# Reordered weight stores and reloads, and an output layer that runs product by product, in a chunked-attention and maxout kernel

## The chip, the cores and the metric

The kernel runs on one core of a Trainium2 chip. The metric is the device time of one execution in microseconds (us), the median of several runs.

The core's engines are named as in the profile: PE (TensorE, matrix products; PEld is its weight load), DVE (VectorE), ACT (ScalarE), POOL (GpSimd) and SP (SyncE). Here SP issues all DMAs, in the order in which they stand in its queue. Each engine works through its own instructions in order, and waits on semaphores for the others.

## The reference

Attention within chunks of 64 positions, for 8 batches, 8 heads, 576 positions and a head dimension of 64; then a maxout layer on all 4608 tokens:

```python
scores = scale * np.matmul(q_c, k_c.transpose(0, 1, 2, 4, 3))
scores = scores - np.max(scores, axis=-1, keepdims=True)
attn = np.exp(scores)
attn = attn / (np.sum(attn, axis=-1, keepdims=True) + 1e-09)
out = np.matmul(attn, v_c)
...
x = np.ascontiguousarray(attn_out.transpose(0, 2, 1, 3)).reshape(B * S, H * D)
...
h = np.maximum(np.maximum(x @ w1, x @ w2), x @ w3)
return (h @ w_out).astype(np.float32)
```

x is 4608 x 512, the hidden width is 768, and the output is 4608 x 512. All is float32.

## The kernel before

**Tiles, groups, units.** The tokens are 36 tiles of 128. The first two groups of four tiles each (`GROUPS`) go through the maxout layer directly, with the weights in SBUF. The other 28 tiles are four units of 7, 8, 7 and 6 tiles (`UNITS`). A unit's tokens are cut into two halves of `count * 64` columns (448, 512, 448, 384).

**Precision.** Each float32 operand is split into a high part, rounded to the matmul's format (`high`, a copy on ACT), and a low part, the difference (`low`, a subtraction on DVE). A product is three matmuls: low by high, high by low, high by high (`product`, L585).

**Seven products.** In a unit, each product of 2 x 2 blocks is made with seven products instead of eight, in the manner of Strassen and Winograd. The operands of the seven are sums and differences of blocks. Those of the weights are made once, during the second group: `store` (L352) for the nine hidden sets, `store_out` (L405) for the three pairs of blocks of the output weights. Both sum on POOL, split on ACT and DVE, and write the originals and the mixed operands to DRAM. Those of the tokens are made per unit: `operands` (L503) for products 1, 2, 5, 6, 7 and `last_operands` (L509) for 3 and 4, into the rooms X1 to X7.

**A unit on PE.** Nine hidden sets (`hidden`, L593), each for two blocks of 128 hidden columns and one of the three weight matrices: seven products in `ORDER` = 1, 6, 5, 2, 7, 3, 4, each of two steps of three matmuls. The results are combined and their maxima over the three matrices kept in M. After every third set the operands Y of the output layer are made from M (L622 to L637). Then comes the output layer (`project`, L644): for each half mm (128 of the 256 output rows of a block), the seven products over three pairs of blocks jp, nine matmuls each; in the first half the steps of products 1, 6 and 5 are interleaved.

**Banks.** There are five PSUM banks for these products. Product 2 goes on accumulating in the bank of product 1, 7 in that of 6, and 3 in that of 5 (`banks_of_product`, L583). So PE may begin product 2 only when the bank's content after product 1 has been read out, and likewise for 7 and 3. In both layers `combine` (L563) has ACT read out 1, 6 and 5 (into `kept`) and 2, and DVE the sums of 7, 3 and 4; POOL makes two further sums.

**Streamed weights.** A set's weights come back from DRAM into two rooms of the ring: originals, 768 KB (`first`, L513), and mixed operands, 1024 KB (`second`, L517). The first room holds the operands of products 1, 2 and 4, the second those of 5, 6, 7 and 3. There are two rooms of each kind, so that set n + 2 is loaded into the rooms of set n. Both loads are planned for just after set n. The output weights come in seven pieces of 768 KB (`load_outer`, L523), each with two successive products of one half, in contiguous rows; pieces 4 to 6 and the next unit's first two sets are loaded during the output layer, each behind every second product (`loads_within`, L873).

**The order of work.** All queues are written out by hand. `FIRST` orders the first group. From then on a clock `now` advances with every step of PE by an assumed duration (`STEP_H`), and every other piece of work has a due time (`plan`, L773); it enters its engine's queue when the clock reaches it (`passed`, L765). The due times set the order only. The steps that matter below: `operands(u + 1, 6.5)` puts the next unit's token operands 6.5 to 15.9 us behind the start of the output layer, `last_operands` comes behind its end, `tiles` (L835) spreads the attention of the unit after next (three PE pieces V, S, T per tile, softmax on the other engines), the first of them `lead` = 20 us behind the start of the output layer.

**Rooms.** `y_room` (L539) places the 21 operands Y. Those of the last pair for products 7, 3 and 4 lie in rooms X3 and X4. `ao` are four rotating rooms for results, each stored to `out_t` by SP.

Of the kernel before, what the change touches and what calls it, by code (L numbers as in the profile page):

```python
# [30 lines left out]
ORDER = (1, 6, 5, 2, 7, 3, 4)  # L31
SOFTMAX = (("mx", 1.0), ("sub", 1.9), ("exp", 2.8), ("sum", 3.8), ("eps", 4.7), ("rec", 4.9), ("nrm", 5.3))
# [30 lines left out]
def chunk_attn_maxout_kernel(  # L63
# [288 lines left out]
    def store(n):  # L352
# [18 lines left out]
        def sum_of(k, x, y, op):  # L371
            def fn():
                if k == 0:
                    st["c"] = att.tile([P, 4, 256], F32, name="c", tag="rv", bufs=1)
                nc.gpsimd.tensor_tensor(out=st["c"][:, k], in0=x(), in1=y(), op=op)
            return fn

        def high():
            st["s"] = xp.tile([P, 2, 4, 256], F32R, name="s", tag=("xh0", "xl0")[n % 2])
            nc.scalar.copy(out=st["s"][:, 0], in_=st["c"])  # L380

        def low():
            nc.vector.tensor_tensor(out=st["s"][:, 1], in0=st["c"], in1=st["s"][:, 0].bitcast(F32), op=minus)  # L383
# [14 lines left out]
        return [(0.0, whole(0, a)), (1.1, whole(1, b)), (2.2, sum_of(0, a21, a22, plus)),  # L398
                (2.9, sum_of(1, sums(0), a11, minus)), (3.6, sum_of(2, a11, a21, minus)),
                (4.3, sum_of(3, a12, sums(1), minus)), (5.3, high), (6.5, low), (9.2, mixed)]  # L400

    place = {i: p for p, i in enumerate(ORDER)}
    outer_w = {}

    def store_out(jp):  # L405
# [24 lines left out]
        def high():  # L430
            st["h"] = late["hold"].tile([P, 4, 256], F32R, name="sh", tag="k0", bufs=1)
            nc.scalar.copy(out=st["h"], in_=st["c"])

        def low():
            st["l"] = late["hold"].tile([P, 4, 256], F32R, name="sl", tag="k1", bufs=1)
            nc.vector.tensor_tensor(out=st["l"], in0=st["c"], in1=st["h"].bitcast(F32), op=minus)

        def to(first, step, many, m, h):
            w = outer_w["w"].rearrange("p (m i j h x) -> p m i j h x", m=2, i=7, j=3, h=2)
            return w[:, m, first:first + step * (many - 1) + 1:step, jp, h]  # L440

        def originals():
            if jp == 0:
                outer_w["w"] = dram.tile([P, 14 * 768], F32, name="wo")
            for h, src in enumerate((woh, wol)):
                for m in range(2):
                    cols = slice(m * P, (m + 1) * P)
                    nc.sync.dma_start(out=to(0, 3, 2, m, h), in_=src[:, j:j + 2, cols].bitcast(F32))
                    cols = slice(256 + m * P, 256 + (m + 1) * P)
                    nc.sync.dma_start(out=to(6, 1, 1, m, h), in_=src[:, j + 1:j + 2, cols].bitcast(F32))  # L450

        def mixed():
            for h, src in enumerate("hl"):
                for m in range(2):
                    cols = slice(m * P, (m + 1) * P)
                    for half in range(2):
                        nc.sync.dma_start(out=to(1 + 3 * half, 1, 2, m, h),
# [511 lines left out]
```

## Time and profile before

| | us |
|---|---|
| median of 3 runs | 634.1 |
| lowest and highest | 631.84, 634.71 |
| the profiled execution: its time | 635.71 |
| its span, first to last instruction | 633.9 |
| DVE busy | 446.6 |
| ACT busy | 277.1 |
| POOL busy | 295.1 |

The profile is of one execution, at full granted clock of TensorE. A row of a timeline gives start, duration, engine, line, operation, output and inputs, and in brackets the idle time before it and what ended it. A row of groups gives count, busy time, mean duration in ns, and the idle time before these instructions with its releasers. A row of windows gives the stretch, then the busy time of PE, PEld, DVE, ACT and POOL with their counts of instructions, the clock, the busy share of the DMA engines and the GB/s that they moved. A DMA row gives the count, the size of one and the median time from issue to landing. The units' places in time: unit 0's hidden sets start at 178.38 us and its output layer at 277.01; the output layers of units 1, 2 and 3 start at 400.87, 515.01 and 608.35.

### The profile page before, as it was taken

How to read it: one execution, taken by the hardware profiler on the slowest of the kernel's cores; microseconds unless marked ns; L12 is line 12 of the kernel's file. 1: busy time of each engine (PE TensorE's matmuls, PEld its weight loads, DVE VectorE, ACT ScalarE, POOL GpSimd, SP SyncE). 2: the span in 40 equal slices, each digit the busy share in tenths (PEclk: the TensorE clock that was granted, in tenths of full speed). 3: DMA queues.
4: the chain of work that ended last, by engine and by line, in shares of the span. 5: the costliest groups of instructions: out<-in, count | busy, mean ns of one | idle time of the engine just before them, and what ended most of it. 6: DMA issues, size and time to landing. Idle time of an engine off the chain costs nothing.

```text
span 633.9 us, 12714 instructions
## 1 busy us (share of the span) xinstructions
PE 614.7 (97%) x5101; PEld 532.6 (84%) x5102; DVE 446.6 (70%) x676; ACT 277.1 (44%) x491; POOL 295.1 (47%) x243
## 2 busy tenths in 40 slices
PE   7899999999999799999999999999999999899997
PEld 3888877878888678999887888888999999899997
DVE  5889854788856786679549596985488567366761
ACT  4888633454534334444434343443243353332341
POOL 2423577765465654356335352552354346243441
PEclk9999999999999999999999999999999999999999
DMA  8988559576958999378774655678665569766675
GB/s 330 362 297 292 199 184 356 205 254 231 347 172 270 300 311 363 120 267 292 292 269 176 245 204 216 226 279 274 269 236 181 202 230 310 269 228 238 233 255 192
DMA packets 52042, 161.26 MB, mean 254 GB/s; under 512 B 5264, under 2 KB 21392, under 8 KB 46224
## 3 DMA queue, kind: packets, MB, share of 16 engines
q1 hardware_dynamic: 51984, 160.45, 70.6%
q8 instruction: 40, 0.66, 0.4%
q14 instruction: 18, 0.15, 0.1%
HBM read 128.97 MB, written 31.46 MB: 253 GB/s over the span
## 4 chain that ended last, share of the span: by engine, by line
PE 73%; DVE 12%; DMA 8%; ACT 4%; issue 2%; POOL 1%; SPq 0%; POOLq 0%; ACTq 0%; DVEq 0%
PE pm L590 55%; DMA ring<-w 5%; PE pm L172 4%; PE pm L173 4%; PE pm L174 4%; PE s L257 2%; DVE X L501 2%; PE tp L245 2%; PE s L222 2%; DMA wo<-sh 2%; DVE e L232 1%; DVE s L383 1%; DVE mx L227 1%; DVE sm L180 1%; ACT e L236 1%
## 5 line engine op out<-in xcount | busy, mean ns | idle before, releaser
L590 PE MATMUL pm<-X,ring 128*128 128x448 f32 (+2 forms) x1584 | 330.8, 365 | 10.1 <-DMA ring<-w 7.6
L590 PEld LDWEIGHTS pm<-X,ring 128*128 128x128 f32 x1584 | 289.6, 188 | 40.8 <-ACT kept L568 3.5
L568 ACT COPY kept<-pm 128x448 f32<-128x448 f32 (+2 forms) x132 | 69.6, 533 | 141.7 <-PE pm L590 114.2
L590 PE MATMUL pm<-Y,ring 128*128 128x448 f32 (+2 forms) x432 | 91.7, 364 | 0.0
L575 POOL TENSOR_TENSOR kept<-kept 128x448 f32<-128x448 f32 (+2 forms) x44 | 55.7, 1266 | 72.2 <-ACT kept L568 71.8
L590 PEld LDWEIGHTS pm<-Y,ring 128*128 128x128 f32 x432 | 79.4, 188 | 7.8 <-DVE Y L626 0.5
L601 DVE TENSOR_TENSOR most<-pm,most 128x448 f32<-128x448 f32 (+2 forms) x72 | 44.6, 620 | 45.7 <-PE pm L590 44.8
L172 PE MATMUL pm<-xh,wl 128*128 128x512 f32 (+1 forms) x156 | 60.8, 390 | 0.0
L189 POOL TENSOR_TENSOR e<-e,sm 128x512 f32<-128x512 f32 x26 | 28.1, 1081 | 67.3 <-DVE sm L186 50.7
L173 PE MATMUL pm<-xl,wh 128*128 128x512 f32 (+1 forms) x156 | 58.4, 374 | 0.3 <-DVE xl L268 0.3
L174 PE MATMUL pm<-xh,wh 128*128 128x512 f32 (+1 forms) x156 | 58.4, 375 | 0.0
L579 POOL TENSOR_TENSOR kept<-kept 128x448 f32<-128x448 f32 (+2 forms) x24 | 30.8, 1283 | 47.8 <-DVE kept L571 42.3
L626 DVE TENSOR_TENSOR Y<-most,Y 128x448 fp32r<-128x448 f32 (+2 forms) x60 | 49.9, 850 | 3.5 <-ACT Y L623 2.9
L571 DVE TENSOR_TENSOR kept<-pm,kept 128x448 f32<-128x448 f32 (+2 forms) x44 | 27.2, 617 | 34.3 <-PE pm L590 30.0
L623 ACT CAST Y<-most 128x448 fp32r<-128x448 f32 (+2 forms) x60 | 33.3, 568 | 23.0 <-DVE most L601 16.0
L227 DVE TENSOR_REDUCE mx<-s 128x8 f32<-128x512 f32 x36 | 24.6, 683 | 22.9 <-PE s L222 22.9
L250 ACT COPY xs<-tp 128x512 f32<-128x512 f32 x36 | 21.0, 584 | 39.4 <-PE tp L245 39.3
L232 DVE TENSOR_TENSOR e<-s,mx 128x512 f32<-128x512 f32 x36 | 24.8, 690 | 17.8 <-ACT stage L271 17.4
L236 ACT ACTIVATE e<-e 128x512 f32<-128x512 f32 x36 | 22.8, 632 | 29.3 <-DVE e L232 29.3
L174 PEld LDWEIGHTS pm<-xh,wh 128*128 128x128 f32 x156 | 29.3, 188 | 5.5
L172 PEld LDWEIGHTS pm<-xh,wl 128*128 128x128 f32 x156 | 29.4, 188 | 5.4
L571 DVE TENSOR_TENSOR pm<-pm,kept 128x448 f32<-128x448 f32 (+2 forms) x48 | 30.1, 627 | 5.2 <-PE pm L590 4.2
(98 smaller groups left out, 859.6 us busy)
## 6 DMA issues: line engine op xcount, KB each, us to landing
ring<-w SPq DMA_DIRECT2D x36, 1024.0 KB, 6.7
ring<-w SPq DMA_DIRECT2D x36, 768.0 KB, 4.7
ring<-wo SPq DMA_DIRECT2D x28, 768.0 KB, 5.3
buf<-in_qk SPq DMA_DIRECT2D x36, 512.0 KB, 6.6
buf<-in_vb SPq DMA_DIRECT2D x36, 256.0 KB, 6.0
w<-s SPq DMA_DIRECT2D x9, 1024.0 KB, 5.4
stage<-in_w SPq DMA_DIRECT2D x7, 512.0 KB, 5.0
out_t<-ao SPq DMA_DIRECT2D x16, 224.0 KB, 4.6
```

The costliest lines, as they stand in the source:

```text
L172: nc.tensor.matmul(out=o, lhsT=al, rhs=bh, start=first, stop=False)
L173: nc.tensor.matmul(out=o, lhsT=ah, rhs=bl, start=False, stop=False)
L174: nc.tensor.matmul(out=o, lhsT=ah, rhs=bh, start=False, stop=last)
L227: nc.vector.tensor_reduce(out=st["mx"].rearrange("p (g c) -> p c g", c=2), in_=st["s"], axis=AX.X, op=ALU.max)
L232: nc.vector.tensor_tensor(out=st["e"].rearrange("p g c k -> p c g k"), in0=st["s"], in1=most.unsqueeze(3).broadcast_to([P, 2, 4, 64]), op= ...
L568: return lambda: nc.scalar.copy(out=kept(k), in_=o[i])
L571: return lambda: nc.vector.tensor_tensor(out=out(), in0=o[i], in1=kept(k), op=plus)
L575: (0.95, lambda: nc.gpsimd.tensor_tensor(out=kept(2), in0=kept(2), in1=kept(0), op=plus))],
L590: nc.tensor.matmul(out=o[i], lhsT=a, rhs=b, start=new and k == 0, stop=last and k == 2, skip_group_check=i in banks_of_product)
L601: return lambda: nc.vector.tensor_tensor(out=M(k, c), in0=of(), in1=M(k, c), op=most)
L623: return lambda: nc.scalar.copy(out=y_room(i, jp)[:, 0, :half], in_=t[i]())
L626: return lambda: nc.vector.tensor_tensor(out=y_room(i, jp)[:, 1, :half], in0=t[i](), in1=y_room(i, jp)[:, 0, :half].bitcast(F32), op=minus)
```

## The change

- Hidden weights lie in DRAM by product, in the order of the products, high beside low. The first room now holds the operands of products 1, 6 and 5, the second those of 2, 7, 3 and 4. Set n + 2 is loaded into the first room behind product 5 of set n, into the second behind product 4.
- `store` writes its originals in rows of 1 KB and its mixed operands in two DMAs instead of one; `store_out` uses five DMAs per pair of blocks instead of twelve, the mixed one with rows of 8 KB.
- The output layer runs product by product in the order `OUTER`, each for both halves m in turn. A piece of output weights holds one product for all three pairs and both halves, in three rows of 2 KB per partition, and each piece's room is loaded anew behind its own product.
- In the output layer ACT reads out 1, 2 and 6; DVE makes the sums of 7, 5, 3 and 4; POOL makes one sum per half. In the hidden layer the combination is as before, written out in `hidden`.
- The operands Y of the last pair lie in other rooms than X3 and X4; `last_operands` is merged into `operands`, and so falls into the output layer (due 15.95 to 18.3 us behind its start). `lead` is 18 instead of 20.
- The order in which the Y operands are made behind a third set is changed: that of product 2 first.

```diff
+OUTER = (1, 2, 6, 7, 5, 3, 4)
...
         def originals():
             stored[n] = dram.tile([P, 14 * 256], F32, name=f"w{n}")
-            for k, src in enumerate((wh[a][:, w], wl[a][:, w])):
-                nc.sync.dma_start(out=stored[n][:, k * 512:(k + 1) * 512], in_=src.bitcast(F32).rearrange("p c x -> p (c x)"))
-            for k, src in enumerate((wh[b][:, w, 2:], wl[b][:, w, 2:])):
-                nc.sync.dma_start(out=stored[n][:, 1024 + k * 256:1280 + k * 256],
-                                  in_=src.bitcast(F32).rearrange("p c x -> p (c x)"))
+            for h, src in enumerate((wh[a], wl[a])):
+                nc.sync.dma_start(out=to()[:, 0:4:3, h], in_=src[:, w].bitcast(F32).rearrange("p (c k) x -> p c (k x)", c=2))
+            for h, src in enumerate((wh[b], wl[b])):
+                nc.sync.dma_start(out=to()[:, 6, h], in_=src[:, w, 2:].bitcast(F32).rearrange("p c x -> p (c x)"))
 
         def mixed():
-            nc.sync.dma_start(out=stored[n][:, 1536:], in_=st["s"].bitcast(F32).rearrange("p a k x -> p (a k x)"))
+            for k in range(2):
+                nc.sync.dma_start(out=stored[n][:, 512 + 1536 * k:1536 + 1536 * k],
+                                  in_=st["s"][:, 2 * k:2 * k + 2].bitcast(F32).rearrange("p i h x -> p (i h x)"))
...
             for h, src in enumerate((woh, wol)):
-                for m in range(2):
-                    cols = slice(m * P, (m + 1) * P)
-                    nc.sync.dma_start(out=to(0, 3, 2, m, h), in_=src[:, j:j + 2, cols].bitcast(F32))
-                    cols = slice(256 + m * P, 256 + (m + 1) * P)
-                    nc.sync.dma_start(out=to(6, 1, 1, m, h), in_=src[:, j + 1:j + 2, cols].bitcast(F32))
+                nc.sync.dma_start(out=to()[:, 0:2, h], in_=src[:, j:j + 2, :256].bitcast(F32))
+                nc.sync.dma_start(out=to()[:, 6, h], in_=src[:, j + 1, 256:].bitcast(F32))
 
         def mixed():
-            for h, src in enumerate("hl"):
-                for m in range(2):
-                    cols = slice(m * P, (m + 1) * P)
-                    for half in range(2):
-                        nc.sync.dma_start(out=to(1 + 3 * half, 1, 2, m, h),
-                                          in_=st[src][:, 2 * half:2 * half + 2, cols].bitcast(F32))
+            nc.sync.dma_start(out=to()[:, 2:6].rearrange("p i h x -> p (i h x)"),
+                              in_=st["s"].bitcast(F32).rearrange("p i h x -> p (i h x)"))
...
-                    (8.3, high(7)), (9.4, low(7))]
-
-        def last_operands():
-            return [(0.0, high(3)), (1.0, low(3)), (1.1, high(4)), (2.2, low(4))]
+                    (8.3, high(7)), (9.4, low(7)), (9.45, high(3)), (10.6, low(3)), (10.7, high(4)), (11.8, low(4))]
...
-                elif p < 4:
-                    pool, tag = ((att, "qs"), (att, "rv"), (late["hold"], "k0"), (late["hold"], "k1"))[p]
+                elif p in (2, 4):
+                    if "k" not in Y:
+                        Y["k"] = late["hold"].tile([P, 2, 2, HALF], F32R, name="Y", tag="k0", bufs=1)
+                    Y[i, jp] = Y["k"][:, p // 2 - 1]
+                elif p == 5:
+                    Y[i, jp] = Y["woh"][:, 0]
+                elif p == 6:
+                    Y[i, jp] = Y[1, 2]
                 else:
-                    Y[i, jp] = rooms["X"]((3, 3, 4)[p - 4])[:, :, (0, 1, 0)[p - 4]]
+                    pool, tag = {0: (att, "qs"), 1: (att, "rv"), 3: (hpool, "h0")}[p]
...
-                after[4] += [(0.2, less(nc.vector, t[5], lambda: M(0, 1), lambda: M(0, 0))), (0.22, t6),
-                             (1.7, less(nc.gpsimd, t[7], lambda: M(1, 1), lambda: M(0, 1))), (2.3, high(6)), (2.6, low(6)),
-                             (2.9, high(5)), (3.4, low(5)), (4.0, high(2)), (4.6, low(2)), (4.7, high(7)), (5.3, low(7)),
-                             (5.35, less(nc.gpsimd, t[4], lambda: M(1, 0), t[6])), (5.4, high(3)), (6.0, low(3)),
-                             (6.7, high(4)), (7.4, low(4))]
+                after[4] += [(0.2, less(nc.vector, t[5], lambda: M(0, 1), lambda: M(0, 0))),
+                             (1.0, less(nc.gpsimd, t[7], lambda: M(1, 1), lambda: M(0, 1))), (1.6, t6), (1.65, high(2)),
+                             (2.4, low(2)), (2.4, high(6)), (3.1, low(6)),
+                             (3.2, less(nc.gpsimd, t[4], lambda: M(1, 0), t[6])), (3.1, high(5)), (3.8, low(5)),
+                             (3.8, high(7)), (4.5, low(7)), (4.9, high(3)), (5.6, low(3)), (5.7, high(4)), (6.4, low(4))]
             for i in ORDER:
                 for k in range(2):
...
-                    yield STEP_H[count], after[i] if k else []
+                    last = [(0.3, loads[i == 4])] if i in (5, 4) else []
+                    yield STEP_H[count], after[i] + last if k else []
...
+            def second(m):
+                return lambda: nc.gpsimd.tensor_tensor(out=kept(2 + m), in0=kept(2 + m), in1=kept(m), op=plus)
+
+            for p, i in enumerate(OUTER):
+                for m in range(2):
+                    after = {1: lambda: [(0.25, copy(m, 1, 0))],
+                             2: lambda: store(m, (0, 0), lambda out, m=m: nc.scalar.copy(out=out, in_=o[m][2])),
+                             6: lambda: [(0.25, copy(m, 6, 2)), (0.95, second(m))],
+                             7: lambda: [(0.25, lambda m=m: sum_of(m, 7, 0)(kept(m)))],
+                             5: lambda: store(m, (1, 1), sum_of(m, 5, 0)),
+                             3: lambda: store(m, (0, 1), sum_of(m, 3, 2)),
+                             4: lambda: store(m, (1, 0), sum_of(m, 4, 0))}[i]()
+                    if m:
+                        after += [(0.3, fn) for fn in loads[p]]
+                    for jp in range(3):
+                        at = m * P
+                        w, y = outer[p][:, jp], y_room(i, jp)
+                        product(o[m], i, w[:, at:at + P], w[:, 256 + at:256 + at + P], y[:, 0, :half], y[:, 1, :half],
+                                jp == 0, jp == 2)
+                        yield STEP_H[count], after if jp == 2 else []
...
-        lead = 14.0 if u == 1 else 20.0
+        lead = 14.0 if u == 1 else 18.0
...
+        behind = [own["load_outer"](4), own["load_outer"](5), own["load_outer"](6)]
+        behind += [nexts[0][0], nexts[0][1], nexts[1][0], nexts[1][1]] if there else [None] * 4
```

In `store`, each result is due 0.25 us behind its product and its DMA to `out_t` 1.0 us behind it.

More of the change, by code (lines that the diff above doesn't have):

```diff
@@ L402, in chunk_attn_maxout_kernel @@
     place = {i: p for p, i in enumerate(ORDER)}
+    place_out = {i: p for p, i in enumerate(OUTER)}
     outer_w = {}
@@ L430, in high, with to @@
         def high():
-            st["h"] = late["hold"].tile([P, 4, 256], F32R, name="sh", tag="k0", bufs=1)
-            nc.scalar.copy(out=st["h"], in_=st["c"])
+            st["s"] = late["hold"].tile([P, 4, 2, 256], F32R, name="so", tag="k0", bufs=1)
+            nc.scalar.copy(out=st["s"][:, :, 0], in_=st["c"])
         def low():
[L435 to L440, printed above, removed]
+            nc.vector.tensor_tensor(out=st["s"][:, :, 1], in0=st["c"], in1=st["s"][:, :, 0].bitcast(F32), op=minus)
+        def to():
+            return outer_w["w"].rearrange("p (j i h x) -> p j i h x", j=3, i=7, h=2)[:, jp]
         def originals():
@@ L591, in product, with hidden @@
                                  skip_group_check=i in banks_of_product)
-        def hidden(n):
+        def hidden(n, loads):
             jp, w = sets[n]
@@ L683, in unit, with store, fn, out @@
-        return dict(operands=operands, last_operands=last_operands, load=load, load_outer=load_outer, hidden=hidden,
+            o = [{}, {}]
+            def store(m, name, make):
+                k, c = name
+                st, at = {}, (t0 - sum(GROUPS)) * P + c * half
+                def fn():
+                    outputs.append(name)
+                    st["o"] = ao_p.tile([P, HALF], F32, name="ao", tag=f"ao{len(outputs) % 4}")[:, :half]
+                    make(st["o"])
+                def out():
+                    nc.sync.dma_start(out=out_t[256 * k + m * P:256 * k + (m + 1) * P, at:at + half], in_=st["o"])
+                return [(0.25, fn), (1.0, out)]
@@ new lines, in copy, with sum_of @@
+            def copy(m, i, k):
+                return lambda: nc.scalar.copy(out=kept(k + m), in_=o[m][i])
+            def sum_of(m, i, k):
+                return lambda out: nc.vector.tensor_tensor(out=out, in0=o[m][i], in1=kept(k + m), op=plus)
+            def second(m):
[17 more added lines that the diff above has]
+                        yield STEP_H[count], after if jp == 2 else []
@@ L684, in unit @@
+        return dict(operands=operands, load=load, load_outer=load_outer, hidden=hidden,
                     project=project)
@@ L867, in load, with loads_behind @@
                 plan(now + t, 0.0, fn)
-    def load_outer(u, *ks):
-        for k in ks:
-            plan(now + 0.3 + 0.3 * (k % 2), 0.0, units[u][0]["load_outer"](k))
+    def loads_behind(u, n):
+        own = units[u][0]
+        if n + 2 < len(sets):
+            return own["load"](n + 2)
+        k = 2 * (n + 2 - len(sets))
+        return own["load_outer"](k + 1), own["load_outer"](k)
     def loads_within(u):
         own, there = units[u][0], u + 1 < len(units)
-        nexts = [units[u + 1][0]["load"](n) for n in range(2)] if there else [((lambda: None),) * 2] * 2
-        return [[own["load_outer"](4)], [own["load_outer"](5)], [own["load_outer"](6)], [nexts[0][1]], [nexts[0][0]],
-                [nexts[1][1]], [nexts[1][0]]]
-    def last_operands(u, begin=0.1):
-        if u < len(units):
-            for at, fn in units[u][0]["last_operands"]():
-                plan(now + begin + at, 0.0, fn)
+        nexts = [units[u + 1][0]["load"](n) for n in range(2)] if there else []
+        behind = [own["load_outer"](4), own["load_outer"](5), own["load_outer"](6)]
+        behind += [nexts[0][0], nexts[0][1], nexts[1][0], nexts[1][1]] if there else [None] * 4
+        return [[fn] if fn else [] for fn in behind]
     def stores_out():
```

125 lines of the change are left out of this document (42 added, 83 removed).

## The prediction

> **What bounds the kernel now.** I read the page first: its busy line, then the matmul group that costs most.
>
> ```profile
> span 633.9 us, 12714 instructions
> ...
> PE 614.7 (97%) x5101; PEld 532.6 (84%) x5102; DVE 446.6 (70%) x676; ACT 277.1 (44%) x491; POOL 295.1 (47%) x243
> ...
> L590 PE MATMUL pm<-X,ring 128*128 128x448 f32 (+2 forms) x1584 | 330.8, 365 | 10.1 <-DMA ring<-w 7.6
> ```
>
> TensorE (PE) is busy in 614.7 of 633.9 us. The change removes no matmul, so all it can win is PE's idle time: 19.2 us in all, of which 10.1 stand before the matmuls of the units. The group view of PE over unit 0's hidden layer, and the timeline of PE, say where these are.
>
> ```profile
> L590 PE MATMUL pm<-X,ring 128*128 128x448 f32 x378 | 80.7, 369 | 8.0 <-DMA ring<-w 5.6 <-ACT kept L568 1.5 <-ACT ao L329 0.9
> ```
>
> ```profile
> 277.01 8.67 PE L590 MATMUL pm<-Y,ring 128*128 128x448 f32 x42
> ...
> 297.77 0.69 PE L257 MATMUL s<-xs,buf 64*64 64x64 f32 x32
> ...
> 299.27 0.86 PE L590 MATMUL pm<-Y,ring 128*128 128x448 f32 x3
> ...
> 400.87 9.81 PE L590 MATMUL pm<-Y,ring 128*128 128x512 f32 x42
> ...
> 515.01 8.67 PE L590 MATMUL pm<-Y,ring 128*128 128x448 f32 x42
> ...
> 549.99 58.51 PE L590 MATMUL pm<-X,ring 128*128 128x384 f32 x336 [1.98 <-DMA ring<-w]
> ```
>
> The first row holds 8.0 us of idle time in unit 0 (178 to 277 us), the last 1.98 us at the start of unit 3. Between them, in units 1 and 2, almost nothing: there the weights arrive in time. The rows also give PE's pace: 42 matmuls in 8.67 us less a tail of 0.37 make 0.203 us each at 448 columns, so 1.82 us for one product of the output layer (nine matmuls), and about 2.07 at 512. A tile put between products costs 299.27 - 297.77 = 1.50 us.
>
> Why are weights late in unit 0? The windows view, the DMA issues within that stretch, and SyncE's (SP's) timeline:
>
> ```profile
> 20.00:40.00 20.00, 19.58 (x207) 17.28 (x206) 17.53 (x36) 17.93 (x35) 5.88 (x5) 1.00 1.00 390
> ...
> 192.00:249.00 57.00, 50.08 (x478) 43.18 (x476) 39.98 (x64) 21.01 (x40) 31.55 (x28) 1.00 0.95 311
> ```
>
> ```profile
> wo<-sh SPq DMA_DIRECT2D x12, 128.0 KB, 9.0
> ```
>
> ```profile
> 206.42 0.37 SPq L515 DMA_DIRECT2D ring<-w  x1
> 206.83 0.43 SPq L519 DMA_DIRECT2D ring<-w  x1
> ...
> 209.66 2.83 SPq L457 DMA_DIRECT2D wo<-sh  x4
> 214.62 5.32 SPq L457 DMA_DIRECT2D wo<-sl  x4
> 219.99 0.68 SPq L519 DMA_DIRECT2D ring<-w  x1
> ```
>
> From 192 to 249 us the DMA engines are 95% busy, yet move 311 GB/s, where they moved 390 when full at 20 to 40. In that stretch SP pushes out the output weights as 36 stores of 64 or 128 KB in rows of 512 bytes. One ring load leaves at 219.99 because eight such stores stand ahead of it from 209.66 on.
>
> **The change part by part.** E is the time at which a unit's output layer begins on PE (277.0, 400.9, 515.0, 608.4).
>
> *Stores of weights.* Hidden sets: `originals` stays at 4 DMAs, in rows of 1 KB; `mixed` goes from 1 to 2. One more issue is 0.41 us of SP (206.42 to 206.83); nine make 3.7 us. I count nothing, as PE works on the second group meanwhile and waits for no DMA there; without that cover it is up to 3.7 us, once. Output weights: 12 stores per pair of blocks become 5 (36 to 15), the mixed one with rows of 8 KB.
>
> *Reloads.* Both rooms of set n+2 are now asked for together after set n; 42 matmuls (8.5 us) later they are wanted, the second after six more (9.7 us). Afterwards the first goes out behind the third product, 24 matmuls earlier (13.4 us of cover), the second at the end of the set, but is first wanted at the fourth product (8.5 + 3.6 = 12.1 us). Loads of the next unit's first sets leave behind products 4 to 7 of the output layer, with 11 to 13 us each, where today the last leaves at its end.
>
> **Gain.** In unit 0 the DMA waits alone are 5.6 us, all idle time there is 8.0; each of the four DMA waits also bares a pipeline tail (0.37 - 0.20 = 0.17 us). The wait of 0.9 for L329 belongs to the second group's output and stays. I take 7.0: the DMA waits with tails (6.3) and half of the copies' 1.5, since those copies run late behind the same traffic. Unit 3's 1.98 with its tail, 2.1, goes too. Sum **9.1 us**, from 5.6 to 10.1 (all but nothing left).
>
> *Outer loads.* Seven of 768 KB per unit remain, in rows of 2 KB instead of 6. Each is issued a product or more earlier than it must land, by 10 us or more; I count nothing. Were one to land 9.0 us after issue, like the 512-byte stores above, it would still be in time.
>
> *Output layer, product by product.* This is where I expect a cost. Today each half mm runs products 1, 6, 5, 2, 7, 3, 4; products 2, 7 and 3 go on in the banks of 1, 6 and 5, after ScalarE (ACT) has copied these. Two products lie between, 3.6 us. Afterwards the order is 1, 1', 2, 2', 6, 6', 7, 7', 5, 5', 3, 3', 4, 4': only one product, 1.82 us, lies between. And bank 5 is read no longer by ACT but by VectorE (DVE), in `store`. Per output layer ACT goes from 8 evacuations to 6, DVE from 6 to 8, GpSimd (POOL) from 4 sums to 2. So PE cannot start product 3 until DVE has reached its sum of 5. How full is DVE at that time?
>
> ```profile
> 277.00:304.50 27.50, 27.50 (x197) 25.23 (x196) 24.97 (x28) 14.71 (x24) 15.44 (x9) 1.00 0.87 315
> ...
> 400.90:431.50 30.60, 30.60 (x197) 25.10 (x196) 26.44 (x30) 14.81 (x24) 16.82 (x9) 1.00 0.85 299
> ...
> 515.00:540.80 25.80, 25.80 (x129) 23.91 (x128) 20.00 (x25) 11.79 (x20) 14.28 (x9) 1.00 0.89 298
> ```
>
> The third busy number is DVE: 24.97 of 27.5, 26.44 of 30.6, 20.0 of 25.8 us, and the change adds two sums and the `low` of X3 and X4 (moved from behind the output layer into it). What stands in DVE's queue ahead of the sum of 5 are the next unit's operands, at plan times E+7.7 (`low` 1) to E+15.9 (`low` 7). DVE's timeline shows when that work is really done:
>
> ```profile
> 285.84 1.21 DVE L501 TENSOR_TENSOR X<-stage,X 128x1024 fp32r<-128x1024 f32 x1
> ...
> 290.98 3.34 DVE L501 TENSOR_TENSOR X<-most,X 128x1024 fp32r<-128x1024 f32 x1 [0.59 <-ACT X L497]
> 294.24 0.61 DVE L571 TENSOR_TENSOR ao<-pm,kept 128x448 f32<-128x448 f32 x1
> ...
> 295.91 4.53 DVE L501 TENSOR_TENSOR X<-stage,X 128x1024 fp32r<-128x1024 f32 x2
> 300.36 0.68 DVE L227 TENSOR_REDUCE mx<-s 128x8 f32<-128x512 f32 x1
> ...
> 411.19 1.08 DVE L501 TENSOR_TENSOR X<-stage,X 128x896 fp32r<-128x896 f32 x1
> ...
> 419.96 4.80 DVE L501 TENSOR_TENSOR X<-stage,X 128x896 fp32r<-128x896 f32 x2
> 424.68 0.68 DVE L227 TENSOR_REDUCE mx<-s 128x8 f32<-128x512 f32 x1
> 426.09 0.69 DVE L232 TENSOR_TENSOR e<-s,mx 128x512 f32<-128x512 f32 x1 [0.73 <-ACT stage L271]
> 427.48 0.69 DVE L180 TENSOR_REDUCE sm<-e 128x8 f32<-128x512 f32 x1 [0.70 <-ACT e L236]
> ...
> 523.84 0.94 DVE L501 TENSOR_TENSOR X<-stage,X 128x768 fp32r<-128x768 f32 x1
> ...
> 531.36 3.47 DVE L501 TENSOR_TENSOR X<-stage,X 128x768 fp32r<-128x768 f32 x2
> ```
>
> `low` 7 ends at E+23.4, E+23.9 and E+19.8: 4 to 7 us behind its plan. Today nobody waits for it. The row at 294.24 is the sum of product 4 of the first half, planned for E+12.85 and run at E+17.2.
>
> Unit 0: ahead of the sum of 5 (planned E+16.45) stand everything up to `low` 7 and two sums instead of three (-0.6). The Y operands before it are reordered and no longer need X rooms, so the chain starts up to 1.4 us earlier; I take 0.7. So 23.4 - 0.6 - 0.7 + 0.6 for the sum itself = E+22.7. PE wants product 3 after ten products and one tile: 18.2 + 1.5 = E+19.7, since a lead of 18.0 falls just there in the plan (30 steps of 0.6003). Stall about 2.5, allowing for the copies of 1 below.
>
> Unit 1 (512 columns): the tile falls before 5' (27 steps of 0.6815), and the sum of 5 comes behind `low` 3 and 4 as well: 23.9 - 2 sums (1.3) - 0.7 + one sum, two `low`, the sum of 5 (0.7 + 2.2 + 0.7) = E+25.5, wanted at 10 x 2.07 + 1.5 = E+22.2. I take 2.5, not the full 3.3, for the two sums DVE can do while POOL holds it up elsewhere. Then the sum of 5' stands behind the tile's maximum, subtraction and sum: 3 x 0.7 plus the two shown waits of 0.7, plus itself, 4.2 us against 2.07 for a product; another 1.5 to 2.1. Together 4.0.
>
> Unit 2: 19.8 - 0.6 - 0.7 + 0.6 = E+19.1 against 18.2 (no tile): 0.7. Unit 3 has no operands to make: 0. Sum 7.2; from 0 (DVE faster by the whole lag) to 12 (rival below).
>
> *Copies of 1.* ACT must copy bank 1 within 1.82 us too, but `high` 2 of Y now stands in ACT's queue just ahead of it (plan E+1.65 against E+2.05), and waits for three DVE steps after the last hidden product.
>
> ```profile
> 279.12 0.57 ACT L623 CAST Y<-m 128x448 fp32r<-128x448 f32 x1 [4.33 <-DVE m L618]
> ...
> 280.31 0.54 ACT L568 COPY kept<-pm 128x448 f32<-128x448 f32 x1 [0.15 <-PE pm L590]
> ```
>
> Today the first such `high` runs at E+2.1. Afterwards its DVE chain is one step longer (0.6), so it starts near E+2.7 and the copy ends near E+3.8, where PE wants the bank at E+3.65: 0.2, more in unit 1, where DVE is later. About 0.4 per unit, four units: 1.5, from 0 to 3.
>
> *At nothing:* ACT's two copies less, POOL's two sums less (neither engine bounds a stage), the rooms of Y. That DVE has `low` 3 and 4 no longer at the next unit's start helps nobody, as PE does not wait there today.
>
> **Sum.** 9.1 gained, 7.2 + 1.5 = 8.7 lost: 0.4 us faster than the profiled execution, whose span is 633.9 and whose time is 635.7. That lies 1.6 above the median of the runs, 634.1, which therefore goes to 633.7; I say **633.5 us**, no change. Half a per cent, 3.2 us, is about what a measurement of this kernel can tell from none.
>
> **The rivals.**
>
> *DVE keeps up.* Today's lag is partly one row: `low` 6 took 3.34 us instead of 1.21. For it: the net work from `low` 1 to the sum of 5 in unit 0 is seven steps of 1.21 and three of 0.61, 10.3 us, which from E+8 would end at E+18.3, before PE asks. Against it: the same overhead (about 4 us) stands in the two other output layers. Then only the copies cost, and at most 1 us of the rest: 634.1 - 9.1 + 1 = 626; with all of unit 0's idle time won 624.
>
> *Slower: POOL holds DVE up longer.* The two long `low` stretches above fall on these POOL rows:
>
> ```profile
> 290.84 2.40 POOL L492 TENSOR_TENSOR stage<-stage 128x1024 f32<-128x1024 f32 x1
> ...
> 296.15 3.20 POOL L492 TENSOR_TENSOR most<-stage,most 128x1024 f32<-128x1024 f32 x1 [2.92 <-ACT kept L568]
> ```
>
> `low` 6 began 0.14 us after POOL's and ended 1.08 us after POOL was done: it stood still meanwhile. The mechanism: POOL's mixes and its two sums of 6 all fall between `low` 1 and the sum of 5, and each holds DVE for its whole length, 2.4 + 3.2 + 2 x 1.2 = 8 us instead of the 4 already in today's times: 4 more in units 0 and 1, 3 in unit 2, so 11 in all, 645; with half of that, 640. It decides once the sum of 5 ends later than about E+24. The Trainium skill ("SBUF — State Buffer", section "Who interferes with whom") states just this: a VectorE instruction with two SBUF inputs and a GpSimd one that reads SBUF exclude each other, and the second to issue waits in full. By that rule the 8 us are the price; the rows at 290.84 and 290.98 agree, while the mean over today's stage says 4.
>
> *The loads stay late.* The engines are 95% busy from 192 to 249 whatever the rows; the same bytes in 8 us less need 311 x 57 / 49 = 362 GB/s, near the 390 seen. Then only SP's queue is eased: 3 us of 7 are won, and with the cost 634.1 - 5.1 + 8.7 = 638. The Trainium skill ("DMA: Bandwidth & Descriptors", section "Specifications") has transfers of 512 bytes and more at full rate; by that the rows of 512 bytes cost nothing, and longer ones win nothing. The two windows above, 311 GB/s at 0.95 and 390 at 1.00, say otherwise, though loads and stores are mixed differently in them.
>
> **Chances and range.** Forecast (gain and cost cancel, 631 to 637): 0.40. DVE keeps up (622 to 630): 0.38. POOL holds DVE (638 to 645): 0.12. Loads stay late (637.5 to 640): 0.10. So faster 0.38, same 0.40, slower 0.22. The range leaves out the last of the first rival and most of the POOL case: 624 to 640; the forecast's own is 631 to 637.
>
> **What would show it.** Right: no wait of PE on ring<-w in unit 0 and at unit 3's start; new waits of PE on DVE's sums into ao, 2 to 5 us at the first two output layers near E+20, none in unit 3; SP's stores of wo in 15 issues. Wrong on the cost: no such waits. Wrong on the gain: PE still waits for ring<-w between 200 and 250 us. What would make the whole wrong is a new wait inside the hidden sets, where the reordered Y work runs during the next set's first products: there a 0.5 us delay would come eight times.

## The result, and the profile after

The changed kernel took 642.7 us (median of 4 runs, 639.1 to 643.6) against 634.2: a ratio of 1.0131, with a 95% interval of 1.0085 to 1.0178. It is slower by 8.5 us, and lies outside the range. The profiled execution took 643.57 us; its span is 641.8 us, 7.9 longer. From the page and the view of PE's waits of the changed kernel (releaser, total us, times, longest; L567 was L590):

```profile
PE 620.8 (97%) x5102; PEld 536.4 (84%) x5102; DVE 445.0 (69%) x684; ACT 269.9 (42%) x483; POOL 277.5 (43%) x235
...
PEclk9999999999999899998999999989999999999999
```

```profile
PE pm L567 <- DVE ao L658: 7.4, 4, 2.9
PE pm L567 <- ACT kept L581: 3.3, 3, 2.1
```

The waits on ring<-w are gone altogether, 7.6 us of them. In their place PE waits 7.4 us for DVE's sums into ao, and 3.3 instead of 1.5 for ACT's copies. PE is also *busy* for 6.1 us longer with the same matmuls: the row of the granted clock (PEclk, in tenths of full speed), all nines before, has three eights in it. Where the longer waits stand, in PE's timeline:

```profile
178.84 2.59 PE L567 MATMUL pm<-X,ring 128*128 128x448 f32 x12
...
218.55 7.91 PE L567 MATMUL pm<-X,ring 128*128 128x448 f32 x30 [2.14 <-ACT kept L581]
...
273.16 18.57 PE L567 MATMUL pm<-Y,ring 128*128 128x448 f32 x90
...
296.27 9.20 PE L567 MATMUL pm<-Y,ring 128*128 128x448 f32 x36 [2.86 <-DVE ao L658]
...
401.54 4.24 PE L567 MATMUL pm<-Y,ring 128*128 128x512 f32 x18
...
422.12 2.32 PE L567 MATMUL pm<-Y,ring 128*128 128x512 f32 x9
427.00 3.92 PE L567 MATMUL pm<-Y,ring 128*128 128x512 f32 x9 [2.56 <-DVE ao L658]
431.25 6.42 PE L567 MATMUL pm<-Y,ring 128*128 128x512 f32 x27 [0.34 <-DVE ao L658]
...
472.41 7.71 PE L567 MATMUL pm<-X,ring 128*128 128x448 f32 x36 [0.98 <-ACT kept L581]
...
522.91 18.56 PE L567 MATMUL pm<-Y,ring 128*128 128x448 f32 x90
543.12 7.55 PE L567 MATMUL pm<-Y,ring 128*128 128x448 f32 x36 [1.65 <-DVE ao L658]
550.51 65.71 PE L567 MATMUL pm<-X,ring 128*128 128x384 f32 x378
616.06 22.36 PE L567 MATMUL pm<-Y,ring 128*128 128x384 f32 x126
```

The rows that begin an output layer (Y at 273.16, 401.54, 522.91, 616.06) cut the span into comparable pieces:

| piece | before, us | after, us | difference |
|---|---|---|---|
| up to unit 0's first set | 178.4 | 178.8 | +0.5 |
| unit 0's nine sets | 98.6 | 94.3 | -4.3 |
| output layer 0 and unit 1's sets | 123.9 | 128.4 | +4.5 |
| output layer 1 and unit 2's sets | 114.1 | 121.4 | +7.2 |
| output layer 2 and unit 3's sets | 93.3 | 93.2 | -0.2 |
| output layer 3 and the end | 25.6 | 25.7 | +0.2 |

Unit 0 wins, as forecast. So does unit 3, where the wait of 1.98 us is gone, but the 1.65 us before it take most of that back. The pieces with the first two output layers lose more than is won. Of their 4.5 and 7.2 us, waits and lowered clock make 4.6 and 5.8 (2.86 + 1.75, and 2.56 + 0.34 + 0.26 + 0.98 + 1.7, as shown below); the 1.4 us left in the second are not explained. Compare the rows at 422.12 and 427.00: nine matmuls took 2.32 us, the same number behind the wait 3.92. The windows view of the changed kernel shows what lies behind it (stretch, busy us of PE, PEld, DVE, ACT, POOL, then granted clock, DMA share, GB/s):

```profile
215.00:220.00 5.00, 2.86 (x12) 2.27 (x12) 4.88 (x6) 4.92 (x11) 4.15 (x5) 0.89 0.99 385
220.00:225.00 5.00, 5.00 (x21) 4.56 (x20) 4.03 (x10) 1.35 (x2) 3.97 (x4) 0.77 0.82 329
...
295.00:300.00 5.00, 3.73 (x13) 3.35 (x14) 4.62 (x6) 0.32 (x2) 0.00 (x0) 0.74 0.55 161
300.00:305.00 5.00, 5.00 (x24) 4.55 (x23) 3.41 (x7) 0.93 (x2) 1.04 (x1) 0.91 1.05 372
...
425.00:430.00 5.00, 3.00 (x7) 2.38 (x8) 3.32 (x6) 1.21 (x2) 0.00 (x0) 0.72 0.43 130
430.00:435.00 5.00, 4.66 (x19) 3.45 (x18) 2.76 (x6) 0.00 (x0) 1.04 (x1) 0.94 0.95 297
```

Behind each of three waits the granted clock falls; in windows of 0.3 us it stands at 0.50, for 3.4 us each time (218.9 to 222.4, 297.4 to 300.9 and 427.1 to 430.6). The loss is 5 x (0.11 + 0.23) = 1.7 us, 5 x (0.26 + 0.09) = 1.75 and 5 x (0.28 + 0.06) = 1.7: together 5.1, which is the 0.8% by which the whole execution's mean clock (0.992) falls short. Of the four runs the one at clock 1.000 took 639.14 us, those at 0.992 took 643.2 and 643.6, the one at 0.995 took 642.2. The clock is not the whole of the loss: in that one execution at full clock the changed kernel still took 5.0 us more than the median before.

And DVE's queue ahead of the sum of product 5, in its timeline (first output layer, then the second):

```profile
291.42 4.26 DVE L498 TENSOR_TENSOR X<-stage,X 128x1024 fp32r<-128x1024 f32 x2
295.61 0.61 DVE L658 TENSOR_TENSOR ao<-pm,kept 128x448 f32<-128x448 f32 x1
...
424.27 1.07 DVE L498 TENSOR_TENSOR X<-stage,X 128x896 fp32r<-128x896 f32 x1
425.26 1.08 DVE L498 TENSOR_TENSOR X<-most,X 128x896 fp32r<-128x896 f32 x1
426.27 0.68 DVE L658 TENSOR_TENSOR ao<-pm,kept 128x512 f32<-128x512 f32 x1
```

The sum ends 0.05 us before PE goes on: at 296.22 (295.61 + 0.61; PE at 296.27) and 426.95 (PE at 427.00). The order is the one that the due times give, `low` 2 and 7 ahead of it in the first layer, `low` 3 and 4 too in the second.

### The profile page after: what moved, and what is told of

The parts are those of the page before. It is cut to its first block, busy times and chain, and to the rows that moved or that the text cites. A ratio compares the mean times of both kernels' runs of the same rounds, so it can differ in the third digit from the quotient of the medians.

```text
span 641.8 us, 12694 instructions
## 1 busy us (share of the span) xinstructions
PE 620.8 (97%) x5102; PEld 536.4 (84%) x5102; DVE 445.0 (69%) x684; ACT 269.9 (42%) x483; POOL 277.5 (43%) x235
## 4 chain that ended last, share of the span: by engine, by line
PE 71%; DVE 17%; ACT 5%; issue 4%; POOL 2%; DMA 1%; SPq 0%; ACTq 0%; DVEq 0%; POOLq 0%
PE pm L567 53%; PE pm L173 4%; PE pm L174 4%; PE pm L175 4%; DVE X L498 3%; PE s L258 2%; PE tp L246 2%; DVE most L578 2%; PE s L223 2%; DVE e L233 2%; DVE mx L228 1%; DVE s L384 1%; DVE sm L181 1%; ACT e L237 1%; ACT stage L272 1%
## 5 line engine op out<-in xcount | busy, mean ns | idle before, releaser
L567 PE MATMUL pm<-X,ring 128*128 128x448 f32 (+2 forms) x1512 | 313.3, 367 | 4.4 <-ACT kept L581 3.3
L567 PEld LDWEIGHTS pm<-X,ring 128*128 128x128 f32 x1512 | 278.2, 189 | 32.4 <-ACT kept L581 5.1
L581 ACT COPY kept<-pm 128x448 f32<-128x448 f32 (+2 forms) x108 | 56.8, 532 | 149.9 <-PE pm L567 129.6
L567 PE MATMUL pm<-Y,ring 128*128 128x448 f32 (+2 forms) x504 | 107.7, 373 | 7.7 <-DVE ao L658 7.4
L567 PEld LDWEIGHTS pm<-Y,ring 128*128 128x128 f32 x504 | 94.4, 193 | 19.9 <-DVE ao L658 9.0
L591 POOL TENSOR_TENSOR kept<-kept 128x448 f32<-128x448 f32 (+2 forms) x36 | 43.5, 1209 | 82.5 <-ACT kept L581 82.3
L614 ACT CAST Y<-most 128x448 fp32r<-128x448 f32 (+2 forms) x72 | 39.6, 571 | 44.4 <-DVE most L578 44.4
L617 DVE TENSOR_TENSOR Y<-most,Y 128x448 fp32r<-128x448 f32 (+2 forms) x72 | 53.8, 777 | 3.0 <-ACT Y L614 1.6
L587 POOL TENSOR_TENSOR kept<-kept 128x448 f32<-128x448 f32 (+2 forms) x24 | 30.5, 1269 | 52.0 <-DVE kept L584 43.2
L584 DVE TENSOR_TENSOR kept<-pm,kept 128x448 f32<-128x448 f32 (+2 forms) x36 | 22.3, 619 | 25.4 <-PE pm L567 21.8
L233 DVE TENSOR_TENSOR e<-s,mx 128x512 f32<-128x512 f32 x36 | 24.8, 690 | 18.3 <-ACT stage L272 17.6
L237 ACT ACTIVATE e<-e 128x512 f32<-128x512 f32 x36 | 22.7, 632 | 27.7 <-DVE e L233 27.7
```

What stands on the lines that cost most here:

```text
L233: nc.vector.tensor_tensor(out=st["e"].rearrange("p g c k -> p c g k"), in0=st["s"], in1=most.unsqueeze(3).broadcast_to([P, 2, 4, 64]), op= ...
L567: nc.tensor.matmul(out=o[i], lhsT=a, rhs=b, start=new and k == 0, stop=last and k == 2, skip_group_check=i in banks_of_product)
L581: return lambda: nc.scalar.copy(out=kept(k), in_=o[i])
L584: return lambda: nc.vector.tensor_tensor(out=out(), in0=o[i], in1=kept(k), op=plus)
L591: (0.95, lambda: nc.gpsimd.tensor_tensor(out=kept(2), in0=kept(2), in1=kept(0), op=plus))],
L614: return lambda: nc.scalar.copy(out=y_room(i, jp)[:, 0, :half], in_=t[i]())
```

## The experiments

Theory A: the change loses because PE waits before product 3 for DVE, and each long wait may be followed by a stretch of lowered clock. Theory B: the waits only stand in for another limit. The others are named where they come up. The runs were made on three chips, on each beside its own runs of the kernel before; so ratios are compared, not times across chips.

**The four late DVE steps behind the sums of 5** (e_operands_later).

```diff
-                    (5.8, low(6)), (5.9, high(2)), (7.0, low(5)), (8.0, mix(4, b21, source[6], nc.gpsimd)), (8.2, low(2)),
-                    (8.3, high(7)), (9.4, low(7)), (9.45, high(3)), (10.6, low(3)), (10.7, high(4)), (11.8, low(4))]
+                    (5.8, low(6)), (5.9, high(2)), (7.0, low(5)), (8.0, mix(4, b21, source[6], nc.gpsimd)), (10.2, low(2)),
+                    (8.3, high(7)), (12.0, low(7)), (9.45, high(3)), (12.6, low(3)), (10.7, high(4)), (13.8, low(4))]
```

> The changed kernel with only the due times of four DVE steps moved: low of X2, X7, X3 and X4 fall behind the sums of product 5, so that DVE reaches these sums in time. Nothing is computed otherwise. Theory A (the change loses because PE waits before product 3 for DVE's sum of 5, and each long wait is followed by about 3.4 us at half clock): PE's waits on DVE's ao sums fall from 7.4 us to under 2, the granted clock near 295 and 428 us goes back to 1.00 (3.4 us), time 630 to 634. Theory B (the waits only stand in for another limit, DVE's total work in the output layer): PE waits as long, but at the next unit's products 2 and 7 for X2 and X7, time 640 to 643.

634.5 us against 632.1, ratio 1.0030 (1.0006 to 1.0054): most of the loss is gone, by due times alone. PE's waits in its profile, which is of the fastest of its ten executions (631.75 us) and shows full clock in the output layers:

```profile
PE pm L567 <- ACT kept L581: 3.5, 3, 2.3
PE pm L567 <- DVE ao L658: 2.1, 1, 2.1
```

Of 7.4 us on DVE one wait of 2.1 is left, in unit 1, where the sum of 5' stands behind a tile's maximum, subtraction and sum and behind two of the moved steps (`low` 3 and 4 at 417.67 and 419.34, 1.08 us each): the new due times put these behind the sum of 5, but not behind that of 5'. The first and third output layers have none, and no new wait for X2 or X7 comes up: theory A, not B. The median is 0.5 us above the expectation's end.

**Product 5 read out by ACT, summed by POOL** (e_act5). `copied` has ACT copy product 5 into the result's room and POOL add `kept(m)` there; then comes the store.

```diff
-                             5: lambda: store(m, (1, 1), sum_of(m, 5, 0)),
+                             5: lambda: copied(m),
```

> The changed kernel, but product 5 is read out by ACT (a copy into the result's room) and the sum added there by POOL, so that the bank no longer waits for DVE; DVE has two sums less per output layer, ACT two copies and POOL two sums more. Theory A: the waits of 7.4 us on DVE go; ACT itself stands behind the high part of X4, which waits for POOL, so 1 to 2.5 us of new waits on ACT remain; time 632 to 637. Theory B (whoever reads 5, the engines are too full there): waits of 5 us or more, 639 to 643.

638.2 us, ratio 1.0086 (1.0062 to 1.0110): between the two ranges. DVE's waits fall to 0.5 us, but in unit 1 a single new one comes up, longer than expected. PE's row, and ACT's before it:

```profile
425.03 8.06 PE L567 MATMUL pm<-Y,ring 128*128 128x512 f32 x27 [3.97 <-ACT ao L669]
```

```profile
422.53 0.58 ACT L272 COPY stage<-s 128x512 f32<-128x512 f32 x1 [3.39 <-DVE mx L228]
423.87 0.63 ACT L237 ACTIVATE e<-e 128x512 f32<-128x512 f32 x1 [0.76 <-DVE e L233]
424.41 0.57 ACT L669 COPY ao<-pm 128x512 f32<-128x512 f32 x1
```

The place is not the expected one. ACT's copy of 5 stands behind the high part of X4, which waits for POOL, and ends at 418.65, yet PE goes through 5' and 3 without a wait. It waits before 3': ACT's copy of 5' (at 424.41) stands behind the tile's softmax, whose two ACT steps wait 3.39 and 0.76 us for DVE. Whichever engine frees the bank, what counts is what stands ahead of it in that engine's queue.

**Work without use in place of the waits** (e_filler, then e_filler_both). The edit shown is that of e_filler_both; e_filler has the extra matmuls for the first half alone.

```diff
-            if first:
+            if first and i not in o:
...
+                        if (i, jp) == (3, 0) and t0 < 23 and m <= (count == 8):
+                            o[m][4] = bank()[:, :half]
+                            for _ in range(10 if m else 14 if count == 7 else 12):
+                                nc.tensor.matmul(out=o[m][4], lhsT=w[:, :P], rhs=y[:, 0, :half], start=True, stop=True)
```

> The changed kernel with 14 (unit 0) and 12 (unit 1) extra matmuls put before product 3, into the bank that product 4 overwrites anyway: work without use that keeps PE busy while it would wait for DVE. Theory A (the lowered clock follows from PE's idling): no clock below 1.00 around 295 and 428 us, and the time falls by up to 3.4 us though work was added, 638.5 to 641. Theory C (the clock drops for another reason, chance or load): clock as before the filler, time 642 to 645.

641.4 us, ratio 1.0150 (1.0118 to 1.0182), no better than the changed kernel: a miss by the expected time of 638.5 to 641, and undecided. The clock stayed at 1.00 in the first output layer; in the second PE now waited 1.9 us before product 3', which had not been filled, and the clock fell there.

> The changed kernel with extra matmuls without use at all three places of the long waits on DVE: 14 before product 3 in unit 0, 12 before 3 and 10 before 3' in unit 1 (with only the first two places filled, the clock dropped behind the third). Theory A (the clock is lowered because PE idles): clock 1.00 from 290 to 310 and from 420 to 440 us, output layers of units 0 and 1 about 1.7 us shorter each than in the changed kernel (32.2 and 36.0). Theory C (chance or load): the clock falls somewhere there all the same.

> The changed kernel itself once more, beside the others on the same chip: 1.013 of the kernel before, with 7 us of waits on DVE and one to three stretches of lowered clock.

These two ran on one chip: 641.7 us, ratio 1.0142 (1.0116 to 1.0167), and for the changed kernel 642.3, ratio 1.0163 (1.0137 to 1.0189), with 9.0 us of waits on DVE in its profile where 7 were expected. By the totals they can't be told apart. The stages can. PE's timeline with all three places filled, and the clock there (second output layer):

```profile
422.00 2.88 PE L680 MATMUL pm<-Y,ring 128*128 128x512 f32 x12
...
426.93 2.44 PE L680 MATMUL pm<-Y,ring 128*128 128x512 f32 x10
429.20 6.33 PE L567 MATMUL pm<-Y,ring 128*128 128x512 f32 x27
435.37 5.63 PE L567 MATMUL pm<-X,ring 128*128 128x448 f32 x27
```

```profile
425.00:430.00 5.00, 5.00 (x23) 4.08 (x23) 3.15 (x7) 1.22 (x2) 0.56 (x1) 1.00 0.90 300
430.00:435.00 5.00, 5.00 (x24) 4.12 (x23) 1.38 (x2) 0.00 (x0) 0.49 (x1) 1.00 0.97 291
```

The same windows of the changed kernel on that chip:

```profile
425.00:430.00 5.00, 3.08 (x14) 2.19 (x13) 2.85 (x6) 1.22 (x2) 1.04 (x1) 0.98 0.98 330
430.00:435.00 5.00, 5.00 (x17) 3.97 (x16) 1.25 (x2) 0.00 (x0) 0.00 (x0) 0.68 0.94 290
```

With PE kept busy, the last 27 matmuls of the layer took 6.33 us at full clock; in the changed kernel beside it 8.08. That layer is 36.1 us long with 22 useless matmuls in it, and 37.7 without (398.66 to 436.32). So in this layer the clock stayed full where PE was kept busy. That is one execution of each. That the lowered clock follows PE's idling rests as much on all the profiles together (last section). In the first layer nothing can be read: the changed kernel waited 2.86 us there as before, and this time kept full clock (the layer took 30.5 us in both). The expected gain of 1.7 us was met, with 1.6, in the second layer only.

**The old order of the Y operands behind the first two sets with maxima** (e_old_y). The list `after[4]` of the kernel before is used for jp < 2 (the first two of a unit's three sets with maxima), the new one for jp = 2.

> The changed kernel, but behind sets 3 and 6 of each unit (the first two of the three sets with maxima) the Y operands are made in the order of the kernel before; only behind the ninth set in the new one. Theory D (the new order puts the high part of Y2, which waits for DVE's last maximum, ahead of ACT's copies, and so causes the waits of 2.1 and 1.0 us at 216 and 471 us and the lowered clock at 220): these waits fall to 1.3 and 0, clock at 220 back to 1.00, time 638 to 641. Rival: the waits come from the shorter unit 0 alone, in which DVE has less time; then no change, 642 to 644.

641.4 us, ratio 1.0143 (1.0122 to 1.0165), between the two ranges: theory D falls for unit 0. PE's timeline:

```profile
219.29 9.12 PE L567 MATMUL pm<-X,ring 128*128 128x448 f32 x30 [3.33 <-ACT kept L581]
```

The wait there is longer with the old order: 3.33 us against 2.14 in the changed kernel, and 2.17 to 2.94 in the six other profiles with the new order and the weights' preparation in its old place. The 0.98 in unit 2 is gone: that one the new order does cause.

**The early reload alone** (e_reload_only): `store`, `load`, `weights` and the reload behind products 5 and 4 from the changed kernel; `store_out` and the output layer as before.

> The kernel before with the new layout and the early reloads of the hidden weights only; output weights (36 stores) and output layer as before. If the early reload by itself wins the time of unit 0: PE's waits on ring<-w in unit 0 fall from 5.6 us to under 1, unit 3's 2 us stays, time 626.5 to 629. Rival (the stores in rows of 512 bytes hold SP and the DMA engines, so loads stay late whatever their place): 3 us or more of these waits stay, time 630 to 634.

629.8 us against 632.1, ratio 0.9970 (0.9951 to 0.9988). All waits on ring<-w are gone, unit 3's too (which was expected to stay), so the rival (512-byte stores keep loads late) is out. But the time misses the expected 626.5 to 629, and one wait on ACT's copies has grown, from 1.3 us:

```profile
PE pm L590 <- ACT kept L568: 3.3, 1, 3.3
```

The spans of the two profiles differ by 6.5 us, the medians by only 2.3. The profiled execution of the kernel before (635.71 us) was slower than each of its four timed ones beside the changed kernel (631.8 to 634.7), so its 7.6 us of waits on ring<-w are likely more than it usually has; no trace of another execution of it was kept.

**The long stores without the early reload** (e_late_reload): the changed kernel with both reloads after the set. The new layout of the rooms stays, and with it the second room is first wanted at the fourth product instead of the second.

```diff
-                    last = [(0.3, loads[i == 4])] if i in (5, 4) else []
+                    last = [(0.3, loads[0]), (0.9, loads[1])] if i == 4 else []
```

> The changed kernel, but both rooms of a hidden set are again reloaded only after the set's end, 0.3 and 0.9 us behind it; the stores of the output weights stay few and long. Theory F (the early reload alone took PE's DMA waits away): waits on ring<-w come back in unit 0, 3 to 6 us, time 643.5 to 648. Theory G (fewer and longer stores are enough): no such waits, time as for the changed kernel, 640 to 643.

641.3 us, ratio 1.0133 (1.0111 to 1.0155), as the changed kernel, and without a single wait on ring<-w: theory G, as far as the early reload is not needed. Whether the fewer stores or the later use of the second room did it is not separated. So either half of the change removes the DMA waits of unit 0; both together remove no more.

**The wait in unit 0's third set.** It stands where Y operands, softmax and the preparation of the output weights meet. Theory H: the preparation's POOL and DVE work makes it. The first new line is that of e_reload_shift and e_all, the second that of e_third_later and e_third_y.

```diff
-                plan(now + 16.0 + 14.0 * jp + at, 0.0, fn)
+                plan(now + (16.0, 28.0, 56.0)[jp] + at, 0.0, fn)
...
+                plan(now + (16.0, 30.0, 56.0)[jp] + at, 0.0, fn)
```

> The kernel before with early reloads (as in e_reload_only), and the preparation of the output weights spread otherwise: its second pair begins 2 us earlier in the plan, its third 12 us later, out of the time in which unit 0's third set makes its Y operands. Theory H (the wait of 3.3 us on ACT's copy in unit 0's third set comes from POOL and DVE being taken by that preparation): the wait falls under 1 us, time 626 to 628. Rival (the third set's own Y work is too much for DVE there): wait stays 2 to 3.3, time 629 to 630.5.

633.7 us, ratio 1.0016 (1.0003 to 1.0028), a miss. The second pair, moved forward by 2 us, runs into the second set's copies: ahead of them ACT now has that pair's rounding (sh, at 209.38), which waits 6.12 us for earlier stores into wo. In PE's timeline:

```profile
210.91 7.88 PE L590 MATMUL pm<-X,ring 128*128 128x448 f32 x24 [6.04 <-ACT kept L568]
...
225.44 6.58 PE L590 MATMUL pm<-X,ring 128*128 128x448 f32 x30 [1.31 <-ACT kept L568]
```

The third set's wait did fall, to 1.31. So the third pair alone was moved:

> As e_reload_only, with only the third pair of the output weights' preparation 12 us later in the plan; the second pair stays where it was (e_reload_shift had also moved it 2 us forward, and a wait of 6.0 us came up in the second set). Theory H (the third pair's sums on POOL and DVE make the wait of 3.3 us in unit 0's third set): that wait falls to about 1.3, none of 6 us comes up, time 626.5 to 629. Rival (any shift only moves the wait): waits on ACT's copies in unit 0 stay at 3 us or more, 629.5 to 633.

627.7 us against 632.4, ratio 0.9932 (0.9908 to 0.9956); the wait is 1.63 us. Theory H holds for the third pair. With the new order of Y in that one set (there its last maximum too is due earlier, at 0.95 instead of 2.7 us, as in the changed kernel):

> As e_third_later, and behind unit 0's third set the Y operands are made in the new order of the changed kernel. If the new order helps there (2.1 us of wait in the changed kernel against 3.3 with the old order): 0.5 to 1 us less than e_third_later. Rival: it puts ACT's copies behind the high part of Y2 and wins nothing.

626.5 us, ratio 0.9918 (0.9887 to 0.9949), faster than both kernels. Its lead of 1.2 us over e_third_later is within the intervals, but the wait is seen to go (0.6 us at 217; the two small ones on ring<-w make 0.7):

```profile
PE pm L590 <- ACT kept L568: 0.8, 2, 0.6
```

**All in the changed kernel** (e_all): the four late steps, lead 20, and the shift of e_reload_shift.

> The changed kernel with the four DVE steps behind the sums of 5 (as in e_operands_later), the lead back at 20 so that unit 1's tile comes behind product 5', and the output weights' preparation spread as in e_reload_shift. Theory A with H: PE's waits on DVE's ao sums under 1 us (7.4 in the changed kernel, 2.1 with the four steps moved alone), on ACT's copies under 1.5, time 625 to 629. Theory B (other limits take their place in the output layers): 631 to 635.

635.6 us, ratio 1.0048 (1.0027 to 1.0069). DVE's waits fall from 7.4 to 1.6 us, near what A asked, but ACT's rise to 4.4. Of these 2.7 stand in unit 0's second set, where ACT's rounding of the moved pair again waits for stores (2.76 us); the shift had failed there by itself. So the time misses A's range, and B's too by 0.6. The new output layer without its waits was not seen to beat the old one anywhere.

## Why the prediction was wrong

**The mechanism of the loss was right, and its size nearly so.** The cost of the output layer was put at 2.5, 4.0 and 0.7 us; PE waited 2.86, 2.56 + 0.34 and 1.65, in all 7.4 against 7.2. The sum of 5 was forecast to end at E+22.7 and E+25.5 and ended at E+23.1 and E+25.4 (296.22 - 273.16 and 426.95 - 401.54). Unit 3 has no such wait, as said. That the totals agree so closely is partly luck: unit 2's wait is more than twice the 0.7, and the second wait of unit 1 is 0.34 instead of 1.5 to 2.1, as product 3 ran at the lowered clock meanwhile. In e_changed, where product 3 had full clock, it was 1.92, and the sum 9.0.

**The step that failed is the sum.** It charged a wait with its own length. Three of the waits were each followed by 1.7 us of lost clock, 5.1 us in the profiled execution, a term that the prediction did not have. Without it the profiled execution would be 2.8 us slower than before, not 7.9, against the 0.4 faster that was forecast; the rest is unit 0's smaller gain (1.0 without the clock), the 1.4 us left unexplained above, and 0.5 lost before unit 0, with small terms both ways. PE waited 3.0 and 2.0 us in the profile of the kernel before with no loss of clock, and nothing in that trace pointed to one. Later executions of the same kernel do: on the chip of e_operands_later 8 of 19 had a mean clock of 0.995 or 0.997, where one loss of 1.7 us makes 0.997. The Trainium skill ("TensorE: Matmul & The Clock Gate", section "What's actually happening") describes a gate that halves TensorE's clock after an idle window of some 3.4 us and needs about as long a busy one to lift it. The 3.4 us at a clock of 0.50 agree with its second half; the page's idle time doesn't, as waits of 2.1 to 2.9 us were enough here. A rule weighed against the plan for new waits would have given this rival a place.

**The gain in unit 0 was too large.** 7.0 us were put down, 4.3 came, and of the missing 2.7 the lowered clock took 1.7. The DMA waits went, as said. The prediction took ACT's late copies for a result of the same traffic and counted half of their 1.5 us as won; in fact the wait in the third set grew from 1.3 to 2.1 (to 3.3 with the old order). The preparation of the third pair of output weights makes about half of it (3.33 to 1.63 in e_third_later); in the kernel before, the DMA wait of 3.04 just ahead had hidden a part.

**Copies of 1** were charged 1.5 us and cost 0.3 (one wait, at 406 us in unit 1). In their place the reordered Y work costs 1.0 in unit 2's hidden sets, the case the prediction named as making the whole wrong, though once and not eight times.

**The rivals.** "DVE keeps up" is out. "POOL holds DVE up longer" names a range in which the time fell, 638 to 645, but by luck: its mechanism did not come. In unit 0 DVE's seven long steps ahead of the sum of 5 lasted 12.7 us in both kernels, 4.2 more than 7 x 1.21; the 8 us would have needed 4 more. "The loads stay late" is out: nothing waited for them. From 192 to 249 us the changed kernel moved 331 GB/s at a DMA share of 0.93, the kernel before 311 at 0.95. How much the rows of 512 bytes held up the loads is not separated; with early reloads the same stores made nothing wait (318 GB/s at 0.95). The stores of the output weights were miscounted: the view of DMA issues has 48 in the kernel before, 16 per pair of blocks and 40 of them from 192 to 249 us, not 36 and 12. The 15 afterwards are right. Unit 3's 2.1 us came as forecast: its wait is gone.

By the table the gain of 9.1 was thus 6.4 (4.3 in unit 0, with 1.7 of lost clock taken off, and 2.1 in unit 3). The cost of 8.7 was 13.8 with the other 3.4 of clock (4.5, 7.2, 1.9 and 0.2 in the four pieces from output layer 0 on, unit 3's gain taken out). With 0.5 us lost before unit 0 that makes +7.9 us instead of -0.4.

## What to carry to other kernels

Before a bank is shared between two products, ask which engine frees it and what is queued ahead there: 2 us of matmuls in between cover a copy on an idle engine, not one behind a queue that runs 7 us late. A late engine behind one wait is only seen when that wait is removed, so look at the next stage's slack before counting the gain. And where a change has two remedies for one wait, try each alone: here either half was enough.

## What the hardware showed that was not expected

The granted clock of TensorE fell to 0.50 behind waits of only 2 to 3 us, and not always. Over the fourteen profiles of this case it fell thirteen times between the first matmul and the last; each fall began less than 1.5 us before or behind the end of a wait of PE of 1.9 us or more. Nine of the twenty waits between 2.1 and 3.4 us had one, both longer ones (4.0 and 6.0 us), and two of the three between 1.9 and 2.0 us; none of 1.7 us or less. One of these two, in e_changed, came 2.3 us of work after a wait of 2.59, so both waits may count there. A fall lost 1.7 us eleven times (3.4 us at half clock) and 3.4 us twice, behind the waits of 3.33 us in e_old_y and of 6.0 us in e_reload_shift. The same wait of 2.86 us in the first output layer cost 1.75 us of clock in one execution of the changed kernel and nothing in another. This makes a part of the spread of the times: 639.1 to 643.6 us for the changed kernel, 631.8 to 638.1 for e_operands_later, where the slowest execution has the lowest clock, 0.992. Why a given wait trips the clock and another doesn't was not tested.
